# An induced-attention and channel-mix kernel with its transposes, stores and first units in another order

## Chip, cores and metric

The kernel runs on one core of one Trainium2 chip. The metric is the device time of one execution in microseconds (us); the time given is the median of several runs. A core has five engines that run side by side and each work through their own instructions strictly in order: TensorE (PE in the profile; its weight loads are PEld), VectorE (DVE), ScalarE (ACT), GpSimd (POOL) and SyncE (SP), which here issues nearly all DMA transfers. They wait for each other through semaphores.

## What is computed

Two layers follow each other, in float32, for 4 batches of 12608 rows of 128 numbers. The first is attention through 32 inducing rows; the second mixes each row with the row before it and sends the mix through a squared ReLU layer with 1024 hidden channels and a sigmoid gate.

```
mab(q, kv) = softmax(scale * q @ kv.T) @ kv        # scale = 1/sqrt(128)
h    = mab(inducing, x)                            # 32 x 128 for each batch
x1   = mab(x, h)                                   # 12608 x 128
prev = x1 moved down by one row, a row of zeros first
xk   = mu_k * x1 + (1 - mu_k) * prev
xr   = mu_r * x1 + (1 - mu_r) * prev
out  = sigmoid(xr @ w_r) * ((max(xk @ w_k, 0) ** 2) @ w_v)
```

## The kernel before, in words

**Stages.** Stage A makes h of a batch: scores of the inducing rows against x, a running maximum, exponentials, and sums. Stage B makes the attention weights of each row of x against h, 32 per row. It never forms x1: the weights of a row (split in a high and a low part, so that they can be multiplied exactly enough in the fast fp32r form) are laid into a tile R, and h is multiplied into w_k and w_r beforehand (`combine`), which gives the tiles W. One product with W[0] and one with W[1] (R moved by one column, for the previous row) then give the hidden layer.

**Units and steps.** The last layer is cut into groups of 512 rows and each group into 4 units of 256 hidden channels: 25 groups x 4 units x 4 batches = 400 units. The main loop takes one step n for each unit. In step n it issues, on each engine's queue in this order: the gate of a group that is done; `up` of unit n (4 matmuls into the PSUM tile ps_a, lines 839 and 841; there are two such buffers); what stands in `early` for this step (`soon`); `zgate` once per group (lines 828 and 829, the product for the sigmoid); `square` (line 851 on DVE: k_t, the ReLU, which reads ps_a; line 856 on ACT or 853 on DVE: kh, the square rounded to fp32r; line 857 on ACT: the exact square; line 859 on POOL: kl, their difference); `store` of a finished group (line 886 on DVE and line 894, its DMAs); `down` of unit n - 4 (6 matmuls, line 870); and last what stands in `events` for this step (`at`). Only lines 853 and 851 free a ps_a buffer, so `up` of step n waits for them from step n - 2. In steps 4 and 8 of a block of 12 (`high_vector`), line 853 on DVE makes kh instead of ACT.

**What runs beside.** All of stage A of the next batch and stage B of later rows is hung into these steps by hand. For each block of 12 steps that begins at step s there is one `stage_a(b + 1, j, at, s)` and one `stage_b(b, j + 1, at, s + 1)`. With the positions of a block (0 to 11): stage A has the four transposes `btr` (line 359, DVE, they read the loaded x block xb) at positions 9, 11, 0 and 3, each pair followed by a DMA to DRAM (line 362) and by `regroup` DMAs back (line 365) at positions 1 and 5; `load_x` of the next block at 5 (line 207); its scores (line 391, PSUM bank pb_a) at 1, and in the block that also takes in the tail of the batch at 9; the sums over x (`hmm`, line 458, pb_a) at 7 and `acc`, which reads them from pb_a (line 473), at 8. Stage B has its scores (line 649, PSUM bank pb_b) at 1, the transpose and the maximum (`trans` line 656, `maxi` line 659) at 2, the subtraction at 3, and later the exponential, the sum, the division, the way back and the DMAs of `spread` (line 702) into R.

**The start.** `head` makes stage A of batch 0 with no layer to hide behind, and the weights wk, wv and wr are converted from their raw form there (`load_weight`: exponent, mantissa, sign, join; the last has two GpSimd operations). `start` then makes stage B of the first four groups in two parts (`stage_b_head`: scores, turn, diff, expo, norm; then `place`: high, low, put) and the parts of W (`wpart`: product, high on ACT, low on DVE, line 566); what isn't needed by the first unit is hung into steps 0 to 6. W's last columns, for the gate, are `wg`; they are first needed by `zgate(first=True)`, hung into step 4. L537 copies h out of PSUM, L523 makes its factor for k1, L116 is the exponent step of a conversion.

Of the kernel before, what the change touches and what calls it, by code (L numbers as in the profile page):

```python
# [8 lines left out]
F32 = mybir.dt.float32  # L9
# [10 lines left out]
def kernel(  # L20
# [11 lines left out]
    nc = tc.nc  # L32
# [134 lines left out]
    def split_wv(c):  # L167
        cs = slice(c * cg, (c + 1) * cg)
        nc.scalar.copy(out=wvh[:, cs, :], in_=wv_sb[:, cs, :])
        nc.gpsimd.tensor_tensor(out=wvl[:, cs, :], in0=wv_sb[:, cs, :], in1=wvh.bitcast(F32)[:, cs, :],  # L170
                                op=ALU.subtract)

# [165 lines left out]
    def stage_a(b, j, at, t):  # L338
# [130 lines left out]
        def acc():  # L469
# [5 lines left out]
            S.xb.pop(j)  # L475

        for c in range(Q):
            at(t + (-3, -1, 0, 3)[c], lambda c=c: btr(c))
            at(t + (1, 1, 5, 5)[c], lambda c=c: regroup(c))
        if tail:  # L480
# [12 lines left out]
        at(t + 19, t_hmm)  # L493
        at(t + 20, acc)
        k = order_a.index((b, j))
        for bn, jn in order_a[k + 1:]:
            if jn < NBLK - 1:
                at(t + 5, lambda: load_x(bn, jn))
                if jn == NBLK - 2:
                    at(t + 5, lambda: load_x(bn, jt))  # L500
                break


    def combine(b, at=None, t=0):
# [20 lines left out]
        def gates():  # L525
            for nm, mu in (("r0", mur), ("r1", omur)):
                if ahead:
                    h4 = L["h4"][nm] = sm.tile([P, P], F32, name="h4" + nm, bufs=1)
                    nc.scalar.activation(out=h4, in_=L["hp"], func=AF.Copy, scale=mu)
                else:  # L530
                    mixed((nm, mu))

        def hfin():
            ps = pb_tile("a" if ahead else "b")
            nc.tensor.matmul(out=ps[:, :P], lhsT=S.acc, rhs=L["sw"], start=True, stop=True)
            h = sm.tile([P, P], F32, name="hT")
            nc.vector.tensor_copy(out=h, in_=ps[:, :P])  # L537
            S.hT = h[:, :M]
            L["hp"] = ps[:, :P]
            L["h4"] = {}  # L540
            if ahead:
                h4 = L["h4"]["k0"] = sm.tile([P, P], F32, name="h4k0", bufs=1)
                nc.scalar.activation(out=h4, in_=L["hp"], func=AF.Copy, scale=muk)
            else:
                mixed(("k0", muk))
            mixed(("k1", omuk))
            if not ahead:
                gates()
            S.W = [wp.tile([P, WF], F32R, name=f"W{s}") for s in range(2)]
# [81 lines left out]
    def stage_b(b, j, at, t, quick=False):  # L631
# [73 lines left out]
        if quick:  # L705
            at(t, scores)
            for n, f in ((1, trans), (1, maxi), (1, sub), (2, total), (2, recip), (3, mult), (3, back), (4, low)):
                at(t + n, f)
            soon(t + 2, expo)
            soon(t + 4, high)  # L710
            for i in range(Q):
                at(t + 5 + i, lambda i=i: spread(i))
            return
        at(t, scores)
        at(t + 1, trans)
        at(t + 1, maxi)
        at(t + 2, sub)
        at(t + 3, expo)
# [94 lines left out]
    class Group:  # L813
# [62 lines left out]

        def store(self):

# [9 lines left out]
            if g % span == span - 1 or g == NG - 1:  # L888
                o0 = (g % UO - g % span) * G
                t0 = (g - g % span) * G  # L890
                dst = out[self.b, t0:t0 + o - o0 + w, :].rearrange("(s q) (j d) -> j q s d", q=M, d=M)
                for i in range(Q):
                    eng = nc.scalar if self.b == B - 1 and g == NG - 1 and i % 2 else nc.sync
                    eng.dma_start(out=dst[i], in_=ot[M * i:M * (i + 1), o0:o + w]
                                      .rearrange("q (s d) -> q s d", d=M))

# [53 lines left out]
    def head():  # L950
# [52 lines left out]
        for c in range(FC // cg):  # L1003
            split_wv(c)
        spin(5)
# [8 lines left out]
        w.acc()  # L1014
        run(conv["r", 0][:2])
        spin(2)
# [12 lines left out]
    def start():  # L1029
# [15 lines left out]
        def gate_bank(s):  # L1045
            if s == 0:
# [7 lines left out]
        S = batches[0]  # L1054
        run([gates, sc0, sc1, tu0, df0, ex0, wa[0][0], wa[1][0], wb[0][0], lambda: spin(2), tu1, nm0, *conv["r", 0][2:], wa[0][1], hi0,
             wa[1][1], wb[0][1], lo0, wa[0][2], put0, lambda: spin(2),
             df1, ex1, wa[1][2], nm1, hi1])
        for n, f in ((0, wb[1][0]), (0, wb[1][1]), (1, lambda: run([w[0] for w in wg])),
                     (1, sc2), (1, put1)):
            soon(n, f)  # L1060
        for n, f in ((0, lo1), (0, wb[0][2]), (0, wb[1][2]), (2, tu2), (2, df2), (2, ex2), (3, nm2)):
            at(n, f)
        for prod, high, low in wg:
            soon(1, high)
            at(1, low)
        for k, (high, low, put) in enumerate(pl1):
# [26 lines left out]
    with tc.manual_schedule():  # L1093
        head()
        start()
        for n in range(len(units) + LAG + 2):
# [5 lines left out]
            if grp is not None:  # L1102
# [4 lines left out]
                low = grp.square(u, n in high_vector)  # L1107
                low(nc.vector if n == end else nc.gpsimd, 0, grp.w)
            if 1 <= m <= len(units) and units[m - 1][1] == NU - 1:
                units[m - 1][0].store()  # L1110
            if old is not None:
# [32 lines left out]
```

## Time and profile before

| | us |
|---|---|
| median of 3 runs (1113.17 to 1113.67) | 1113.23 |
| profiled execution | 1114.14 |
| its span, first to last instruction | 1111.9 |
| ACT busy in the span | 966.5 |
| POOL busy in the span | 951.7 |

A line of the order of time has the start and the duration in us, the engine, the line of the kernel, the operation, output and inputs, how many such instructions in a row, and in brackets the idle time of the engine before it with what ended it. In the view of waits a line has the engine and the line that waited, the engine and line for which it waited, the total in us, how often, and the longest.

### The profile page before, as it was taken

Reading aid. Unit: us, or ns where it says so; the run is one execution under the profiler, and the core shown is the slowest. Engines: PE = TensorE matmul, PEld = TensorE weight load, DVE = VectorE, ACT = ScalarE, POOL = GpSimd, SP = SyncE. Lnnn points to the kernel's source line nnn. Section 1 sums busy time; section 2 is a strip of 40 time slices with the busy share of each in tenths; the row PEclk is TensorE's granted clock in tenths of the full one; section 3 lists DMA queues with packets and bytes.
Section 4 is the critical chain, followed back from the end, with each engine's and each line's share of the span. In section 5 each row is a group of like instructions: output and inputs, shape, how many; then the busy total and the mean of one; then the engine's idle time right before and its main releaser. Section 6 shows DMA issues by size and latency. Waiting matters only on the chain.

```text
span 1111.9 us, 17188 instructions
## 1 busy us (share of the span) xinstructions
PE 1088.7 (98%) x5723; PEld 832.8 (75%) x5723; DVE 907.3 (82%) x1287; ACT 966.5 (87%) x1098; POOL 951.7 (86%) x417
## 2 busy tenths in 40 slices
PE   8899999999999999999999999999999999999997
PEld 6577777777777777777787777777777787777886
DVE  6988888986878899887778888888676888887665
ACT  6698889889889888888898988979889998999995
POOL 3388998898898988889888999879898899999997
PEclk9999999999999999999999999999999999999999
DMA  9045655661356556653235646655223132232212
GB/s 343 10 127 120 171 147 145 155 167 25 62 135 150 154 148 152 146 152 82 48 78 151 167 119 149 160 138 133 41 55 73 36 66 58 55 70 57 45 29 35
DMA packets 256247, 121.10 MB, mean 109 GB/s; under 512 B 221440, under 2 KB 224672, under 8 KB 253856
## 3 DMA queue, kind: packets, MB, share of 16 engines
q1 hardware_dynamic: 255152, 119.92, 45.2%
q8 instruction: 45, 0.74, 0.3%
q14 instruction: 42, 0.34, 0.1%
q10 hardware_dynamic: 1008, 0.10, 0.1%
HBM read 46.94 MB, written 44.70 MB: 82 GB/s over the span
## 4 chain that ended last, share of the span: by engine, by line
PE 71%; DVE 13%; ACT 4%; issue 3%; DMA 2%; POOL 0%; SPq 0%; DVEq 0%; ACTq 0%; POOLq 0%
PE ps_v L870 35%; PE ps_a L839 14%; PE ps_a L841 13%; DVE k_t L851 6%; PE pb_b L649 2%; ACT kh L856 2%; DVE kh L853 2%; PE pb_a L458 2%; PE pb_a L391 2%; PE ps_v L828 2%; PE ps_v L829 2%; DMA R<-R 1%; DVE s L656 1%; DVE oT L875 1%; ACT k_t L857 1%
## 5 line engine op out<-in xcount | busy, mean ns | idle before, releaser
L859 POOL TENSOR_TENSOR kl<-k_t,kh 128x1024 fp32r<-128x1024 f32 (+1 forms) x399 | 937.3, 2384 | 122.1 <-ACT k_t L857 101.0
L851 DVE TENSOR_SCALAR k_t<-ps_a 128x1024 f32<-128x1024 f32 (+1 forms) x400 | 479.1, 1198 | 142.0 <-PE ps_a L841 115.9
L857 ACT ACTIVATE k_t<-k_t 128x1024 f32<-128x1024 f32 (+1 forms) x400 | 418.4, 1048 | 34.1 <-DVE kh L853 23.0
L856 ACT ACTIVATE kh<-k_t 128x1024 fp32r<-128x1024 f32 (+1 forms) x352 | 365.2, 1038 | 82.7 <-PE ps_v L870 41.6
L839 PE MATMUL ps_a<-R,W 128*128 128x512 f32 (+1 forms) x800 | 323.5, 405 | 8.6 <-DVE k_t L851 4.5
L841 PE MATMUL ps_a<-R,W 128*128 128x512 f32 (+1 forms) x800 | 313.5, 392 | 0.0
L870 PE MATMUL ps_v<-kh,wvh 128*128 128x512 f32 (+1 forms) x800 | 248.4, 391 | 0.0
L870 PE MATMUL ps_v<-kl,wvh 128*128 128x512 f32 (+1 forms) x800 | 247.3, 390 | 0.9 <-POOL kl L859 0.3
L870 PE MATMUL ps_v<-kh,wvl 128*128 128x512 f32 (+1 forms) x800 | 246.8, 390 | 0.0
L839 PEld LDWEIGHTS ps_a<-R,W 128*128 128x128 f32 x800 | 150.8, 188 | 76.7 <-DVE kh L853 10.6
L870 PEld LDWEIGHTS ps_v<-kl,wvh 128*128 128x128 f32 x800 | 148.1, 188 | 38.2 <-POOL kl L859 6.9
L870 PEld LDWEIGHTS ps_v<-kh,wvh 128*128 128x128 f32 x800 | 149.6, 188 | 34.2
L870 PEld LDWEIGHTS ps_v<-kh,wvl 128*128 128x128 f32 x800 | 149.6, 188 | 34.1
L841 PEld LDWEIGHTS ps_a<-R,W 128*128 128x128 f32 x800 | 150.4, 188 | 30.6 <-issue 0.2
L875 DVE TENSOR_TENSOR oT<-ps_v,rT 128x512 f32<-128x512 f32 (+1 forms) x100 | 66.6, 666 | 1.8
L886 DVE STREAM_TRANSPOSE ot<-oT 128x512 f32<-128x512 f32 x96 | 67.2, 700 | 0.0
L853 DVE SCALAR_TENSOR_TENSOR kh<-ps_a,k_t 128x1024 fp32r<-128x1024 f32 x48 | 58.8, 1224 | 5.0
L359 DVE STREAM_TRANSPOSE xs<-xb 128x512 f32<-128x512 f32 x72 | 50.0, 694 | 11.7 <-DMA xb<-in_x_dram 11.7
L831 ACT ACTIVATE rT<-ps_v 128x512 f32<-128x512 f32 (+1 forms) x99 | 57.8, 584 | 0.3
L831 ACT ACT_TABLE_LOAD x31 | 39.8, 1283 | 0.5
L828 PE MATMUL ps_v<-R,W 128*128 128x512 f32 (+1 forms) x99 | 39.1, 395 | 0.4 <-DVE oT L875 0.4
L829 PE MATMUL ps_v<-R,W 128*128 128x512 f32 (+1 forms) x99 | 38.9, 393 | 0.0
(217 smaller groups left out, 607.7 us busy)
## 6 DMA issues: line engine op xcount, KB each, us to landing
out_dram<-ot SPq DMA_DIRECT2D x184, 128.0 KB, 3.3
xb<-in_x_dram SPq DMA_DIRECT2D x18, 1024.0 KB, 6.8
xd<-xs SPq DMA_DIRECT2D x36, 512.0 KB, 3.1
xt<-xd SPq DMA_DIRECT2D x72, 256.0 KB, 4.2
R<-ah SPq DMA_DIRECT2D x184, 64.0 KB, 2.1
R<-al SPq DMA_DIRECT2D x184, 64.0 KB, 2.1
kl<-in_x_dram SPq DMA_DIRECT2D x4, 512.0 KB, 8.8
xb<-in_x_dram SPq DMA_DIRECT2D x4, 512.0 KB, 11.1
```

The source lines that it names most:

```text
L828: nc.tensor.matmul(out=ps[:, :w], lhsT=S.W[0][:, F:WF], rhs=R[:, 1:w + 1], start=True, stop=False)
L831: nc.scalar.activation(out=self.rT, in_=ps[:, :w], func=AF.Sigmoid)
L839: nc.tensor.matmul(out=ps[:, c, :w], lhsT=S.W[0][:, cs], rhs=R[:, 1:w + 1], start=True, stop=False)
L841: nc.tensor.matmul(out=ps[:, c, :w], lhsT=S.W[1][:, cs], rhs=R[:, 0:w], start=False, stop=True)
L851: nc.vector.tensor_scalar(out=k, in0=self.ps[:, :, :w], scalar1=0.0, scalar2=None, op0=ALU.max)
L853: nc.vector.scalar_tensor_tensor(out=kh, in0=self.ps[:, :, :w], scalar=0.0, in1=k, op0=ALU.max, op1=ALU.mult)
L856: nc.scalar.activation(out=kh, in_=k, func=AF.Square)
L857: nc.scalar.activation(out=k, in_=k, func=AF.Square)
L859: return lambda eng, a, z: eng.tensor_tensor(out=kl[:, :, a:z], in0=k[:, :, a:z], in1=kh.bitcast(F32)[:, :, a:z], op=ALU.subtract)
L870: nc.tensor.matmul(out=self.v, lhsT=wt[:, fc, :], rhs=kk[:, c, :], start=(fc == 0 and n == 0), stop=(fc == FC - 1 and n == 2))
L875: nc.vector.tensor_tensor(out=self.oT, in0=self.v, in1=self.rT, op=ALU.mult)
L886: nc.vector.transpose(out=ot[:, o:o + w], in_=self.oT)
```

## The change

Six things change places; the arithmetic is the same, but for who computes two of the factors.

- Stage B: `trans` and `maxi` are issued in the same step as the scores, and `sub` one step earlier. In its quick form (used twice, at the first and second batch's start) the first two also move a step ahead, and all from `total` on comes a step later.
- Stage A: `load_x` is issued before the `btr` and `regroup` of its step; the first `btr` comes a step later (position 10); for the first block of the second batch all `btr` come later (steps 5, 5, 6, 9 in place of 1, 3, 4, 7) and `regroup` two steps later. `acc` comes a step later, at position 9.
- The DMAs of `store` are issued two steps after their transpose, but for the last two groups, which send at once.
- The last unit's kl, on DVE, is issued two steps later.
- In the head, GpSimd's subtraction for wvl and the conversion of wr come later, the factors r0 and r1 are made by GpSimd from h in SBUF, not by ACT from PSUM, and k0 by ACT from SBUF.
- In the start the order is another: the scores of the first part come before the gate factors, W's low parts of the second half come before `lo1`, the gate parts `wg` are multiplied in step 2 (before: 1), and their high and low parts come in step 3 (before: 1).

```diff
--- before.py
+++ after.py
@@ -166,9 +166,14 @@
 
     def split_wv(c):
         cs = slice(c * cg, (c + 1) * cg)
-        nc.scalar.copy(out=wvh[:, cs, :], in_=wv_sb[:, cs, :])
-        nc.gpsimd.tensor_tensor(out=wvl[:, cs, :], in0=wv_sb[:, cs, :], in1=wvh.bitcast(F32)[:, cs, :],
-                                op=ALU.subtract)
+
+        def high():
+            nc.scalar.copy(out=wvh[:, cs, :], in_=wv_sb[:, cs, :])
+
+        def low():
+            nc.gpsimd.tensor_tensor(out=wvl[:, cs, :], in0=wv_sb[:, cs, :], in1=wvh.bitcast(F32)[:, cs, :],
+                                    op=ALU.subtract)
+        return high, low
 
     def groups(j):
 
@@ -474,9 +479,16 @@
                                                in1=L["hp"][:, :C], op0=ALU.mult, op1=ALU.add)
             S.xb.pop(j)
 
+        k = order_a.index((b, j))
+        for bn, jn in order_a[k + 1:]:
+            if jn < NBLK - 1:
+                at(t + 5, lambda: load_x(bn, jn))
+                if jn == NBLK - 2:
+                    at(t + 5, lambda: load_x(bn, jt))
+                break
         for c in range(Q):
-            at(t + (-3, -1, 0, 3)[c], lambda c=c: btr(c))
-            at(t + (1, 1, 5, 5)[c], lambda c=c: regroup(c))
+            at(t + ((1, 1, 2, 5) if t < SEG else (-2, -1, 0, 3))[c], lambda c=c: btr(c))
+            at(t + ((3, 3, 7, 7) if t < SEG else (1, 1, 5, 5))[c], lambda c=c: regroup(c))
         if tail:
             at(t + 5, t_tr)
             soon(t + 11, t_scores)
@@ -491,14 +503,7 @@
         at(t + 19, lambda: hmm(0))
         at(t + 19, lambda: hmm(1))
         at(t + 19, t_hmm)
-        at(t + 20, acc)
-        k = order_a.index((b, j))
-        for bn, jn in order_a[k + 1:]:
-            if jn < NBLK - 1:
-                at(t + 5, lambda: load_x(bn, jn))
-                if jn == NBLK - 2:
-                    at(t + 5, lambda: load_x(bn, jt))
-                break
+        at(t + 21, acc)
 
 
     def combine(b, at=None, t=0):
@@ -526,7 +531,7 @@
             for nm, mu in (("r0", mur), ("r1", omur)):
                 if ahead:
                     h4 = L["h4"][nm] = sm.tile([P, P], F32, name="h4" + nm, bufs=1)
-                    nc.scalar.activation(out=h4, in_=L["hp"], func=AF.Copy, scale=mu)
+                    nc.gpsimd.tensor_tensor(out=h4, in0=L["h"], in1=mu.broadcast_to([P, P]), op=ALU.mult)
                 else:
                     mixed((nm, mu))
 
@@ -536,11 +541,11 @@
             h = sm.tile([P, P], F32, name="hT")
             nc.vector.tensor_copy(out=h, in_=ps[:, :P])
             S.hT = h[:, :M]
-            L["hp"] = ps[:, :P]
+            L["hp"], L["h"] = ps[:, :P], h
             L["h4"] = {}
             if ahead:
                 h4 = L["h4"]["k0"] = sm.tile([P, P], F32, name="h4k0", bufs=1)
-                nc.scalar.activation(out=h4, in_=L["hp"], func=AF.Copy, scale=muk)
+                nc.scalar.activation(out=h4, in_=h, func=AF.Copy, scale=muk)
             else:
                 mixed(("k0", muk))
             mixed(("k1", omuk))
@@ -704,17 +709,17 @@
 
         if quick:
             at(t, scores)
-            for n, f in ((1, trans), (1, maxi), (1, sub), (2, total), (2, recip), (3, mult), (3, back), (4, low)):
+            for n, f in ((0, trans), (0, maxi), (1, sub), (3, total), (3, recip), (4, mult), (4, back), (5, low)):
                 at(t + n, f)
             soon(t + 2, expo)
-            soon(t + 4, high)
+            soon(t + 5, high)
             for i in range(Q):
-                at(t + 5 + i, lambda i=i: spread(i))
+                at(t + 6 + i, lambda i=i: spread(i))
             return
         at(t, scores)
-        at(t + 1, trans)
-        at(t + 1, maxi)
-        at(t + 2, sub)
+        at(t, trans)
+        at(t, maxi)
+        at(t + 1, sub)
         at(t + 3, expo)
         at(t + 5, total)
         at(t + 5, recip)
@@ -874,7 +879,7 @@
             self.oT = mp.tile([P, G], F32, name="oT", bufs=1)[:, :self.w]
             nc.vector.tensor_tensor(out=self.oT, in0=self.v, in1=self.rT, op=ALU.mult)
 
-        def store(self):
+        def store(self, n):
 
             g, w = self.g, self.w
             if g == NG - 1:
@@ -889,10 +894,18 @@
                 o0 = (g % UO - g % span) * G
                 t0 = (g - g % span) * G
                 dst = out[self.b, t0:t0 + o - o0 + w, :].rearrange("(s q) (j d) -> j q s d", q=M, d=M)
-                for i in range(Q):
-                    eng = nc.scalar if self.b == B - 1 and g == NG - 1 and i % 2 else nc.sync
-                    eng.dma_start(out=dst[i], in_=ot[M * i:M * (i + 1), o0:o + w]
-                                      .rearrange("q (s d) -> q s d", d=M))
+                final = self.b == B - 1 and g == NG - 1
+
+                def send():
+                    for i in range(Q):
+                        eng = nc.scalar if final and i % 2 else nc.sync
+                        eng.dma_start(out=dst[i], in_=ot[M * i:M * (i + 1), o0:o + w]
+                                          .rearrange("q (s d) -> q s d", d=M))
+
+                if self.b == B - 1 and g >= NG - 2:
+                    send()
+                else:
+                    at(n + 2, send)
 
 
     def run(th):
@@ -1001,7 +1014,7 @@
         load_x(1, 0)
         w.expo()
         for c in range(FC // cg):
-            split_wv(c)
+            split_wv(c)[0]()
         spin(5)
         v.etrans()
         v.sums()
@@ -1012,7 +1025,6 @@
         weights()
         w.hmm(1)
         w.acc()
-        run(conv["r", 0][:2])
         spin(2)
         hfin()
 
@@ -1052,17 +1064,19 @@
         wg = [wpart(s, None, lambda s=s: gate_bank(s)) for s in range(2)]
         assert F // G == 2
         S = batches[0]
-        run([gates, sc0, sc1, tu0, df0, ex0, wa[0][0], wa[1][0], wb[0][0], lambda: spin(2), tu1, nm0, *conv["r", 0][2:], wa[0][1], hi0,
-             wa[1][1], wb[0][1], lo0, wa[0][2], put0, lambda: spin(2),
-             df1, ex1, wa[1][2], nm1, hi1])
-        for n, f in ((0, wb[1][0]), (0, wb[1][1]), (1, lambda: run([w[0] for w in wg])),
-                     (1, sc2), (1, put1)):
+        wlow = [split_wv(c)[1] for c in range(FC // cg)]
+        rexp, rman, rsign, rjoin = conv["r", 0]
+        run([sc0, gates, rexp, sc1, tu0, df0, ex0, wa[0][0], wa[1][0], wb[0][0], lambda: spin(2), tu1, nm0, wa[0][1],
+             hi0, rman, rsign, wa[1][1], wb[0][1], lo0, put0, lambda: spin(2), wa[0][2], wa[1][2], df1, rjoin, *wlow,
+             ex1, nm1, hi1])
+        for n, f in ((0, wb[1][0]), (0, wb[1][1]), (1, sc2), (1, put1), (2, lambda: run([w[0] for w in wg]))):
             soon(n, f)
-        for n, f in ((0, lo1), (0, wb[0][2]), (0, wb[1][2]), (2, tu2), (2, df2), (2, ex2), (3, nm2)):
+        for n, f in ((0, wb[0][2]), (0, wb[1][2]), (0, lo1),
+                     (2, tu2), (2, df2), (2, ex2), (3, nm2)):
             at(n, f)
         for prod, high, low in wg:
-            soon(1, high)
-            at(1, low)
+            soon(3, high)
+            at(3, low)
         for k, (high, low, put) in enumerate(pl1):
             at(3, high)
             at(4, low)
@@ -1105,9 +1119,12 @@
                 if n >= NU and u == 1:
                     grp.zgate()
                 low = grp.square(u, n in high_vector)
-                low(nc.vector if n == end else nc.gpsimd, 0, grp.w)
+                if n < end:
+                    low(nc.gpsimd, 0, grp.w)
             if 1 <= m <= len(units) and units[m - 1][1] == NU - 1:
-                units[m - 1][0].store()
+                units[m - 1][0].store(n)
+            if n == end + 2:
+                low(nc.vector, 0, units[end][0].w)
             if old is not None:
                 old.down(ou)
             run(events.pop(n, []))
```

## The prediction

> **What bounds the kernel now.** I read the page first, then the waits, then the order of time at the places that the change touches. The page says that TensorE's row is full almost everywhere:
> ```profile
> span 1111.9 us, 17188 instructions
> PE 1088.7 (98%) x5723; PEld 832.8 (75%) x5723; DVE 907.3 (82%) x1287; ACT 966.5 (87%) x1098; POOL 951.7 (86%) x417
> ```
> A busy PE is not a PE at its pace, so the question is where matmuls come later than they could. The waits view names two waits of the matmuls that cost something; both are for DVE to free the PSUM tile ps_a (columns: total us, times, longest):
> ```profile
> PE ps_a L839 <- DVE k_t L851: 4.5, 4, 1.5
> PE ps_a L839 <- DVE kh L853: 3.4, 12, 0.4
> ```
> So the changed order can win only what DVE's lateness costs PE, plus what the two ends of the span hold. One stall of the second kind, in order of time (start, duration); I call units "steps", and count positions 0 to 11 within a block of 12 steps:
> ```profile
> 420.33 1.23 DVE L851 TENSOR_SCALAR k_t<-ps_a 128x1024 f32<-128x1024 f32 x1 [1.34 <-PE ps_a L841]
> ...
> 422.47 0.72 DVE L656 STREAM_TRANSPOSE s<-pb_b 128x512 f32<-128x512 f32 x1
> ...
> 423.22 0.70 DVE L659 TENSOR_REDUCE pb_b<-s 128x16 f32<-128x512 f32 x1
> ...
> 428.07 1.23 DVE L853 SCALAR_TENSOR_TENSOR kh<-ps_a,k_t 128x1024 fp32r<-128x1024 f32 x1
> ...
> 428.43 0.63 PE L870 MATMUL ps_v<-kl,wvh 128*128 128x512 f32 x2
> ...
> 429.35 0.49 PE L839 MATMUL ps_a<-R,W 128*128 128x512 f32 x1 [0.29 <-DVE kh L853]
> ```
> DVE first idles 1.34 us at position 2, then runs stage B's transpose and maximum, arrives late at position 4, where it has k_t and kh to make, and position 6's first matmul waits for kh's end. Two L870 matmuls take 0.63 together and one alone shows 0.40, so the pace is 0.23 and the last matmul's modelled end hides 0.16 of each stall: 429.35 - 428.43 - 2 x 0.23 = 0.46.
>
> **The change, part by part.**
>
> *Stage B's transpose and maximum one step earlier.* They now stand behind the scores (L649) of position 1. Scores end as position 2's matmuls begin, so DVE does this 0.72 + 0.70 in the 1.34 us in which it idled; k_t of position 2 starts up to 0.3 late, and kh of position 4 is ready about 1.1 us sooner, against a lateness of 0.46. The stall should go in every block: 12 times by the row above, 3.4 + 12 x 0.16 = 5.3 us. Bounds: 0 if DVE finds a new wait in their place, 5.3 if none. I take -5.3. The added wait (transpose for scores) holds k_t, store and expo's inputs behind it on DVE; k_t of position 2 has more than a step of slack before ps_a's other buffer is wanted, so nobody is late by 0.3.
>
> *Loads before regroups, stores two steps later, btr of chunk 0 one step later.* The two longest stalls sit where a block's first transpose waits for its x block:
> ```profile
> 477.62 0.62 PE L870 MATMUL ps_v<-kl,wvh 128*128 128x512 f32 x2
> 477.91 0.71 DVE L359 STREAM_TRANSPOSE xs<-xb 128x512 f32<-128x512 f32 x1 [3.31 <-DMA xb<-in_x_dram]
> ...
> 479.79 0.50 PE L839 MATMUL ps_a<-R,W 128*128 128x512 f32 x1 [1.54 <-DVE k_t L851]
> ```
> ```profile
> 748.23 0.49 PE L839 MATMUL ps_a<-R,W 128*128 128x512 f32 x1 [1.11 <-DVE k_t L851]
> ```
> and SP shows why the load was late:
> ```profile
> 458.77 0.34 SPq L362 DMA_DIRECT2D xd<-xs  x1
> 464.15 3.89 SPq L894 DMA_DIRECT2D out_dram<-ot  x4
> 468.13 1.07 SPq L365 DMA_DIRECT2D xt<-xd  x2
> 469.30 0.38 SPq L207 DMA_DIRECT2D xb<-in_x_dram  x1
> ```
> The load is issued behind four stores (which wait for their transpose on DVE) and two regroups. After the change it stands ahead of both, up to 469.30 - 464.15 = 5 us sooner, and its reader comes a step later. Both cover the 3.31 us. Gain: 1.54 + 1.11 + 2 x 0.16 = 3.0 us; if only the step helps, still most of it. What moves on SP: regroups behind a 1 MB load. It is issued about 8.6 us before it is read in these rows (469.30 to 477.91), and a regroup issued behind it is wanted four steps on at the soonest; no loss taken. The stores themselves have two step times more to land and a buffer that is wanted again 12 steps later: nothing.
>
> *acc one step later.* In the block that also takes in the tail, acc falls into the very step in which the tail block's scores want the same bank, pb_a. Before, it was a step ahead:
> ```profile
> 505.86 0.34 DVE L473 SCALAR_TENSOR_TENSOR acc<-acc,alpha,pb_a 128x128 f32<-128x128 f32 x1
> ...
> 506.12 1.22 DVE L851 TENSOR_SCALAR k_t<-ps_a 128x1024 f32<-128x1024 f32 x1
> ...
> 507.25 0.70 DVE L886 STREAM_TRANSPOSE ot<-oT 128x512 f32<-128x512 f32 x1
> 507.38 1.07 PE L391 MATMUL pb_a<-xt,indT 128*32 128x512 f32 x8
> ```
> Now DVE has k_t (from about 505.95, as acc no longer precedes it), the store's transpose, then acc: 505.95 + 1.22 + 0.70 + 0.34 = 508.2 and a semaphore. Scores that started at 507.38 start at 508.3: PE stands 0.9 us, once in each of the three batches that are prepared: +2.7. Bounds 0 (DVE as early as it can be) and 1.3 each (DVE 0.4 later).
>
> *The end.* The last kl (2.10 us on DVE) no longer stands before the last full group's gate and transpose:
> ```profile
> 1102.47 2.10 DVE L859 TENSOR_TENSOR kl<-k_t,kh 128x640 fp32r<-128x640 f32 x1 [1.64 <-ACT k_t L857]
> ...
> 1104.93 0.45 PE L870 MATMUL ps_v<-kl,wvh 128*128 128x320 f32 x2
> ...
> 1106.02 0.49 DVE L875 TENSOR_TENSOR oT<-ps_v,rT 128x320 f32<-128x320 f32 x1
> 1106.55 0.51 DVE L886 STREAM_TRANSPOSE aT<-oT 128x320 f32<-128x320 f32 x1
> ...
> 1107.99 1.10 SPq L894 DMA_DIRECT2D out_dram<-aT  x2
> ```
> PE ends at 1105.38, but the last gate starts at 1106.02, behind the earlier group's gate and transpose; it can start 0.6 sooner. The last stores of SP start 0.9 after the transpose's end (1107.06), behind the earlier group's four DMAs, which now go out long before: together 1107.99 - 1106.5 = 1.5. Bounds -0.6 and -1.5; I take -1.5, since SP's row is the last issue. I leave kl's own end where it is.
>
> *Head and first steps.* The head gets shorter, and then a new wait eats it:
> ```profile
> 38.09 0.49 PE L535 MATMUL pb_a<-mk,acc 128*128 128x128 f32 x2
> ...
> 39.08 0.28 DVE L537 COPY hT<-pb_a 128x128 f32<-128x128 f32 x1
> ...
> 48.00 0.41 DVE L795 TENSOR_TENSOR al<-pb_b,al 128x256 fp32r<-128x256 f32 x1
> 48.45 0.69 DVE L566 TENSOR_TENSOR W<-pb_a,W 64x512 fp32r<-64x512 f32 x1
> ...
> 51.76 0.50 DVE L566 TENSOR_TENSOR W<-ps_v,W 64x128 fp32r<-64x128 f32 x2
> ...
> 53.66 0.47 PE L839 MATMUL ps_a<-R,W 128*128 128x512 f32 x1 [1.39 <-DVE k_t L851]
> ...
> 54.67 0.40 PE L828 MATMUL pb_a<-R,W 128*128 128x512 f32 x1
> ...
> 55.60 0.40 ACT L767 ACTIVATE s<-s 128x256 f32<-128x256 f32 x1
> ...
> 57.34 0.43 DVE L777 TENSOR_TENSOR pb_b<-s,pb_b 128x256 f32<-128x256 f32 x1
> ```
> hT waited 39.08 - 38.58 = 0.5 us for w_r's conversion, which now comes later; the first units start about 0.6 sooner. But the gate weights' low parts (0.50, at 51.76) move to step 3, on DVE behind norm's last operation (L777), which needs the exponentials of step 2 from ACT. PE's first gate product (L828), in step 4, needs those low parts and stands in PE's order before every later matmul. Norm ended at 57.34 + 0.43 = 57.77. The 0.6 from the head is mostly lost on the way, as lo1 (0.41) now comes behind two lows of 0.69 and put1 and its copy on ACT wait for it; I take 0.4 sooner: 57.4, then 0.50: the gate product starts at 57.9 instead of 54.67, +3.2 us. Step 4's own matmuls (53.66) come about 0.7 sooner, which only lengthens the wait: PE is idle some 3.6 us. What is got back: the stalls that PE had until step 16, which with PE later no longer bind, such as
> ```profile
> 77.24 0.47 PE L839 MATMUL ps_a<-R,W 128*128 128x512 f32 x1 [0.43 <-DVE k_t L851]
> ```
> 0.43 + 0.16 there, and about as little elsewhere: +3.2 - 0.9 = +2.3. Bounds: -0.6 (no wait) to +3.2. The gates' factors go from ACT to GpSimd, and wvl's subtraction to behind the conversion, in a stretch where GpSimd has no other work: nothing. The first batch's four transposes and the quick stage B move by a step or more into steps that, with PE later, have the time; their rows of R are due at step 16, five steps after the last of them is made: nothing.
>
> **Sum:** -5.3 - 3.0 + 2.7 - 1.5 + 2.3 = -4.8. The span of 1111.9 becomes 1107.1; the profiled execution took 1114.14, 0.9 above the median of 1113.23, and against the median the forecast is 1108.4. I count as the same what lies within 0.2% (2.2 us, about what a measurement of this kernel can tell): 1111.0 to 1115.4.
>
> **Rivals.**
>
> *The gate product does not wait* (ACT's exponentials come so early that norm and the lows are done by step 4, or PE has other work). Against it: L777 ended 3.1 us after L828 began. Time: -4.8 - 2.9 = 1105.5. Chance 0.12.
>
> *The idle of 3.6 us costs clock.* The granted clock in windows over the end (third figure from the end of each line):
> ```profile
> 1107.00:1108.00 1.00, 0.00 (x0) 0.00 (x0) 0.06 (x1) 0.00 (x0) 0.00 (x0) 1.00 0.74 117
> 1108.00:1109.00 1.00, 0.00 (x0) 0.00 (x0) 0.00 (x0) 0.00 (x0) 0.00 (x0) 0.83 0.99 142
> ```
> After PE's last matmul (1105.38) the clock fell within 1108 to 1109: 0.83 is one third of that microsecond at half, so 3.3 us after. A gap of 3.6 us in step 4 is just long enough. If matmuls then run at half speed for as long again, 3.3 us of work are 1.6 us late: 1110.0. [...] Chance 0.12.
>
> *Slower: DVE's queue becomes the bound.* The transpose waits at the head of DVE's queue for scores that PE issues last in its step; if it holds k_t of position 2 more than about 0.7 us beyond what I count, kh of position 4 is as late as before and -5.3 is lost: 1113.7. From there every further 0.1 us per block costs 0.1 x 15 blocks: 0.3 more is +4.5, 1118.2. Against it:
> ```profile
> 87.20:219.60 132.40, 131.22 (x698) 98.59 (x697) 118.33 (x164) 114.17 (x128) 114.54 (x49) 1.00 0.59 149
> ```
> in four blocks (87.2 to 219.6) DVE's busy time, the third of the busy times, is 118.33 of 132.40: 3.5 us a block are free. For it: DVE serves in order, so free time at the wrong place is worth nothing. Chance 0.12, half of it above 1115.4.
>
> **Chances.** The forecast 0.64, with its own range 1106 to 1111 from the bounds of acc (0 to 1.3 each), end and head. Faster by over 0.2% has nine tenths of the forecast, the first rival and most of the second: 0.78; the same 0.14; slower 0.08. The range 1104.2 to 1112.8 leaves out the far ends of the first and the third rival.
>
> **What would show it.** Right: the wait of L839 on kh L853 down from 12 times to 3 or fewer; no wait of xs on the x load over 1 us; a wait of L391 for acc three times, near 0.8 each; L828's first row near 58, with PE idle before it and the low parts (L566, 64x128) just before; the last SP store about 1.5 us nearer to PE's last matmul. Wrong: blocks of 12 steps still 33.1 us long (132.40 / 4), or a first gate product on time.

## The result, and the profile after

| | us | runs |
|---|---|---|
| before, median | 1113.45 (1113.17 to 1114.73) | 4 |
| after, median | 1104.92 (1104.70 to 1105.09) | 4 |
| after, profiled execution | 1105.09, its span 1103.3 | |

The ratio is 0.9921, 95% interval [0.9904, 0.9938]: the change takes 8.5 us away, where 5.1 (against this median) were forecast. Line numbers of the kernel after are 5 higher than before for most lines (839 is 844, 870 is 875), 8 for the stores (894 is 902). First the head of the page after, and its chain of work that ended last, by engine:

```profile
span 1103.3 us, 17166 instructions
PE 1083.2 (98%) x5723; PEld 837.2 (76%) x5723; DVE 911.1 (83%) x1287; ACT 967.4 (88%) x1096; POOL 952.9 (86%) x419
...
PE 91%; DVE 4%; ACT 2%; issue 1%; POOL 1%; DMA 1%; POOLq 0%; SPq 0%; DVEq 0%; ACTq 0%
```

TensorE has the same 5723 matmuls and a share of 98% as before; its busy time says nothing of the gain. The waits do:

```profile
DVE s L661 <- PE pb_b L654: 12.0, 24, 1.2
...
PE pb_a L833 <- DVE W L571: 3.2, 1, 3.2
...
PE ps_a L844 <- DVE kh L858: 0.3, 1, 0.3
```

The twelve waits for kh are one. No matmul waits for k_t any more, and no transpose of x waits for its load. In their place stand two new ones: DVE waits 24 times for stage B's scores (first line, the wait that the change added), behind which no matmul is seen to wait, and TensorE waits once, 3.2 us, for the gate's low parts. (A third new wait, for acc, stands in the view under another name; its experiment below shows it.) The block shown before looks like this in the order of time (the steps are those of 420.33 to 429.35 before):

```profile
418.28 0.72 DVE L661 STREAM_TRANSPOSE s<-pb_b 128x512 f32<-128x512 f32 x1 [0.17 <-PE pb_b L654]
419.03 0.69 DVE L664 TENSOR_REDUCE pb_b<-s 128x16 f32<-128x512 f32 x1
419.64 1.21 DVE L856 TENSOR_SCALAR k_t<-ps_a 128x1024 f32<-128x1024 f32 x1
...
426.02 1.22 DVE L858 SCALAR_TENSOR_TENSOR kh<-ps_a,k_t 128x1024 fp32r<-128x1024 f32 x1
```

DVE works without a gap from 418.28 to k_t, where it had idled 1.34 us and then been late. kh is done at 427.24, and the first matmul of position 6, due near 428.0, finds the buffer free.

Where the 8.6 us of the span went, from the starts of the steps' first matmuls in the two traces:

| | before | after | difference |
|---|---|---|---|
| step 0 | 45.48 | 44.82 | -0.66 |
| step 4 | 53.66 | 52.99 | -0.67 |
| step 5 | 56.54 | 60.40 | +3.86 |
| step 16 | 87.21 | 90.99 | +3.78 |
| step 160 | 479.79 | 476.11 | -3.68 |
| step 399 | 1099.15 | 1091.11 | -8.04 |
| end of the span | 1111.9 | 1103.3 | -8.6 |

So the start loses 3.8, steps 16 to 399 win 11.8, and the end wins 0.6. The traced execution of the kernel before took 1114.14, 0.7 above its median, so the spans differ by a little more than typical ones do. On the other side the device time goes beyond the span by 2.2 us before and by 1.8 after: 0.4 of the 8.5 lies outside the span, and no run here shows why.

### The profile page after: what moved, and what is told of

Read it like the earlier page. It is cut to its first block, busy times and chain, and to the rows that moved or that the text cites. A ratio compares the mean times of both kernels' runs of the same rounds, so it can differ in the third digit from the quotient of the medians.

```text
span 1103.3 us, 17166 instructions
## 1 busy us (share of the span) xinstructions
PE 1083.2 (98%) x5723; PEld 837.2 (76%) x5723; DVE 911.1 (83%) x1287; ACT 967.4 (88%) x1096; POOL 952.9 (86%) x419
## 4 chain that ended last, share of the span: by engine, by line
PE 91%; DVE 4%; ACT 2%; issue 1%; POOL 1%; DMA 1%; POOLq 0%; SPq 0%; DVEq 0%; ACTq 0%
PE ps_v L875 47%; PE ps_a L844 17%; PE ps_a L846 16%; PE ps_v L833 2%; PE pb_b L654 2%; PE ps_v L834 2%; PE pb_a L463 2%; PE pb_a L396 2%; ACT kh L861 1%; POOL kl L864 1%; DVE k_t L856 1%; DMA xl<-in_x_dram 1%; DVE mx L263 0%; PE pb_a L583 0%; ACT k_t L862 0%
## 5 line engine op out<-in xcount | busy, mean ns | idle before, releaser
L836 ACT ACTIVATE rT<-ps_v 128x512 f32<-128x512 f32 (+1 forms) x99 | 57.9, 585 | 0.4
```

The source lines that it names most:

```text
L836: nc.scalar.activation(out=self.rT, in_=ps[:, :w], func=AF.Sigmoid)
```

## The experiments

**Theory:** DVE's order in the blocks was the bound; stage B's transposes win most of the time, the loads some, and acc and the gate product give some of it back. **Rivals:** the gain comes from the loads and stores and the transposes are only along; or the start's new order wins and the wait in it is only seen. Each kernel starts from the kernel after, unless it is said otherwise. The ratios are against the kernel before, which was timed again beside them in three groups: its median was 1112.83 us beside the transposes (undone, and alone), acc and the early gate product, 1113.25 beside loads and stores both undone, the filled wait, the old start and all together, and 1112.78 beside the last three (stores at once, load put back, all four stores on SP). The kernel after was timed only beside 1113.45, so a difference from its 1104.92 is uncertain by up to 0.7 us, the spread of these medians.

**The transposes: undone, and done alone.** Undone in the kernel after:

```diff
-        at(t, trans)
-        at(t, maxi)
-        at(t + 1, sub)
+        at(t + 1, trans)
+        at(t + 1, maxi)
+        at(t + 2, sub)
```

> The changed kernel with stage B's transpose, maximum and subtraction one step later again (not in the quick form). Theory: the stall of position 6 (0.46 us, and 0.1 at the restart) comes back in each full block and the blocks between batches lose too: blocks of 33.0 in place of 32.5, in all 6 to 9 us more, 1111 to 1114. Rival: the gain is of the earlier loads and later stores, and the blocks stay at 32.5: within 1.5 us of 1104.9.

Measured: 1114.18 (10 runs, 1113.97 to 1115.72), ratio 1.0011 [1.0002, 1.002]. Without this one part the change is no gain at all, and its trace has the old wait back (13 times in the view of waits):

```profile
PE ps_a L844 <- DVE kh L858: 3.7, 13, 0.3
```

The same three lines the other way round, as the only edit of the kernel before:

```diff
-        at(t + 1, trans)
-        at(t + 1, maxi)
-        at(t + 2, sub)
+        at(t, trans)
+        at(t, maxi)
+        at(t + 1, sub)
```

> The kernel before with stage B's transpose, maximum and subtraction one step earlier (not in the quick form) and nothing else. Theory: full blocks of 32.5 in place of 33.1, the two waits for the x load stay (34.7 and 34.3 become about 34), no gate stall: 6 to 8 us less than 1113.4, 1105.5 to 1107.5. Rival: the blocks need the later stores, too, and the time falls by less than 2.

Measured: 1102.91 (1101.75 to 1105.22), ratio 0.9913 [0.9898, 0.9928]. Three lines alone win 9.9 us, more than the whole change and more than the 1105.5 to 1107.5 expected. The first rival falls. Of the two long stalls for an x load only one is left in its profiled execution (the 1105.22), and it is a costly one:

```profile
736.30 0.71 DVE L359 STREAM_TRANSPOSE xs<-xb 128x512 f32<-128x512 f32 x1 [4.06 <-DMA xb<-in_x_dram]
...
738.18 0.50 PE L839 MATMUL ps_a<-R,W 128*128 128x512 f32 x1 [1.82 <-DVE k_t L851]
...
739.41 1.05 PE L870 MATMUL ps_v<-kh,wvh 128*128 128x512 f32 x2
```

The last row shows two matmuls in 1.05 where 0.63 is usual: the granted clock was 0.98 in the window 738 to 739, 0.50 from 739 to 742 and 0.82 in 742 to 743, so it was at half from 738.96 to 742.37. Stall and clock together would make a spread of 3.5 us if they come in some executions and not in others; only this one was traced.

**Loads and stores: both undone, and each.** The load behind the regroups, the first transpose a step earlier and the stores at once:

```diff
-        k = order_a.index((b, j))
...
-            at(t + ((1, 1, 2, 5) if t < SEG else (-2, -1, 0, 3))[c], lambda c=c: btr(c))
+            at(t + ((1, 1, 2, 5) if t < SEG else (-3, -1, 0, 3))[c], lambda c=c: btr(c))
...
+        k = order_a.index((b, j))
...
-                if self.b == B - 1 and g >= NG - 2:
-                    send()
-                else:
-                    at(n + 2, send)
+                send()
```

> The changed kernel with the x loads behind the regroups again, the first btr a step earlier again, and the stores sent at once. Theory of the prediction: the waits of btr for the x load come back (they cost 3.0 us at steps 160 and 260 before): about 1107.9. Rival, after the run in which only stage B was moved (1101.75 to 1105.22, one such wait in its profile): the earlier transposes on DVE end most of those waits by themselves, the time rises by 0 to 2 and spreads by some us from run to run.

Measured: 1106.69 (6 runs, 1105.43 to 1108.93), ratio 0.9942 [0.9926, 0.9958], 1.8 us above the kernel after and spread over 3.5 us, where that has 0.4. (The slowest, 1108.93, had a granted clock of 0.945, the others 0.997, so the top of this spread may have another cause.) The wait is back:

```profile
DVE xs L364 <- DMA xb<-in_x_dram: 12.3, 6, 3.6
```

Then the stores alone sent at once (the last five lines of this diff):

> The changed kernel with the stores sent at once again; the loads' place and the later first transpose stay as changed. Of the 1.8 us that undoing loads and stores together cost: if the loads' place alone is what takes the wait for the x block away, this kernel is within 0.4 us of the changed one and shows no wait of xs for the x load over 1 us. Rival: the four stores ahead of the load on SP are what made it late, wherever the load stands in its step; then the stalls near 476 and 742 are back and it is 1 to 2 us slower.

And the load and the first transpose alone put back (the lines above them):

> The changed kernel with the load behind the regroups and the first transpose one step earlier again; the stores stay two steps later. If the loads' place is what counts, the stalls near 476 and 742 are back and it is 1 to 2 us slower than the changed kernel; if the stores are, it is within 0.4 us of it. If each alone suffices, both this kernel and the one with the stores at once stay within 0.4 us.

Measured: stores at once 1105.92 (1105.03 to 1106.92), ratio 0.9938 [0.9926, 0.9951]; load put back 1104.80 (1104.64 to 1105.74), 0.9929 [0.9917, 0.9942]. In neither trace is there a wait for the x load: either edit alone removes it. But the first has a new wait, at 251.36, where the tail block's scores are due:

```profile
PE pb_a L396 <- DMA xt<-xd: 1.8, 1, 1.8
```

The regroups, now behind four stores and a 1 MB load, land too late for the scores: the load lands at 249.83, the two regroups at 250.56 and 251.22. In the kernel after they land at 246.14 and 246.88, and the same scores stand 0.58 us. So with the stores two steps later the load's place brings nothing that the runs show (1104.80 against 1104.92). With the load first, the stores' delay is worth 1.0 by the medians, little more than that uncertainty; the traces put 1.2 into the one block of this wait (steps 64 to 76 take 35.64 against 34.39 in the kernel after) and almost nothing into the other blocks.

**acc one step earlier again:**

```diff
-        at(t + 21, acc)
+        at(t + 20, acc)
```

> The changed kernel with acc one step earlier again (as before the change). Theory: the three waits of the tail block's scores (L396, 0.74 us each at 249.1, 504.3 and 768.7) go and nothing takes their place: 2.2 us less, about 1102.7. Rival: acc at the earlier place delays k_t after the kh step on DVE by 0.35 us in each of some 15 blocks, and the time stays at 1104.9 or rises by up to 2.

Measured: 1102.82 (1102.68 to 1102.91), ratio 0.9909 [0.9893, 0.9926]: 2.1 us less than the kernel after. The three blocks with a tail show why; here the second of them in the kernel after:

```profile
503.24 0.70 DVE L891 STREAM_TRANSPOSE ot<-oT 128x512 f32<-128x512 f32 x1
503.86 0.30 DVE L478 SCALAR_TENSOR_TENSOR acc<-acc,alpha,pb_a 128x128 f32<-128x128 f32 x1
```
```profile
503.07 0.62 PE L875 MATMUL ps_v<-kl,wvh 128*128 128x512 f32 x2
504.27 1.07 PE L396 MATMUL pb_a<-xt,indT 128*32 128x512 f32 x8 [0.57 <-PE ps_v L875]
```

acc ends at 504.16 and the scores start 0.11 later. Their start is 0.74 us late (504.27 - 503.07 - 2 x 0.23), three times. The profile names TensorE's own product as releaser; the order of time and the experiment name acc.

**The gate product: earlier, and its wait filled.** The view of the start in the kernel after:

```profile
53.77 0.39 PE L846 MATMUL ps_a<-R,W 128*128 128x512 f32 x1
57.41 0.49 PE L833 MATMUL pb_a<-R,W 128*128 128x512 f32 x1 [3.25 <-DVE W L571]
58.02 0.88 PE L875 MATMUL ps_v<-kh,wvh 128*128 128x512 f32 x2
58.69 1.05 PE L875 MATMUL ps_v<-kh,wvl 128*128 128x512 f32 x2
```
```profile
56.60 0.43 DVE L782 TENSOR_TENSOR pb_b<-s,pb_b 128x256 f32<-128x256 f32 x1
57.06 0.50 DVE L571 TENSOR_TENSOR W<-ps_v,W 64x128 fp32r<-64x128 f32 x2
```

The low parts stand behind norm's last operation, as forecast. After the wait the matmuls run at about half pace (two take 0.88, then 1.05, where 0.63 is usual), and the windows show the granted clock at 0.50 (third figure from the end):

```profile
57.00:58.00 1.00, 0.59 (x2) 0.48 (x3) 0.94 (x4) 1.00 (x2) 1.00 (x1) 1.00 0.00 0
58.00:59.00 1.00, 1.00 (x4) 0.82 (x3) 0.97 (x2) 0.98 (x4) 1.00 (x2) 0.60 0.00 0
...
61.00:62.00 1.00, 1.00 (x5) 0.79 (x4) 0.00 (x0) 0.97 (x2) 0.00 (x0) 0.69 0.00 0
```

The gate's products, high and low parts back in step 1:

```diff
-        for n, f in (..., (1, sc2), (1, put1), (2, lambda: run([w[0] for w in wg]))):
+        for n, f in (..., (1, lambda: run([w[0] for w in wg])), (1, sc2), (1, put1)):
...
-            soon(3, high)
-            at(3, low)
+            soon(1, high)
+            at(1, low)
```

> The changed kernel with the gate parts of W (product, high, low) back in step 1. Theory: PE's wait of 3.25 us before the first gate product (L833) and the clock at half from 58.2 to 61.6 both come from the low parts standing behind norm on DVE in step 3; both go, 3.3 + 1.7 = 5 us less some 1 us of stalls that come back: about 1101, and step 16 begins 4 us sooner than the changed kernel's 90.99. Rival: the steps to 16 are bound by ACT and DVE anyway (ACT was busy nearly without a gap there before), and the time stays within 1 us of 1104.9.

Measured: 1101.87 (1101.64 to 1101.99), ratio 0.9901 [0.9886, 0.9916], 3.05 less than the kernel after; the wait is gone, the granted clock of the profiled execution is 0.999 (0.997 in the kernel after), and step 5 starts at 56.05. The second rival falls: the wait is paid for. To split the wait from the clock, the wait stays and 24 products of the identity fill it; they add matmuls that nobody reads:

```diff
+        soon(4, lambda: spin(12, bank().rearrange("p (a n) -> p a n", a=2)))
```

> The changed kernel with 24 dummy matmuls of 128 columns (2.6 us, results not used) between the matmuls of step 4 and the first gate product, so that PE has work in the 3.25 us in which it stands. Theory: the wait itself stays (first gate product near 57.4) but the clock is not cut at 58.2, so the matmuls after it run at 0.23 and not 0.43: 1.6 us less than 1104.9, 1103.3. Rival: the clock falls for another reason than the idle time, or what it costs is hidden behind ACT: within 0.5 us of 1104.9.

Measured: 1103.30 (1103.15 to 1103.45), ratio 0.991 [0.9895, 0.9925], 1.6 less than the kernel after.

```profile
53.95 2.84 PE L960 MATMUL ps_v<-ident 128*128 128x128 f32 x24
57.37 0.50 PE L833 MATMUL pb_a<-R,W 128*128 128x512 f32 x1 [0.57 <-DVE W L571]
57.97 0.63 PE L875 MATMUL ps_v<-kh,wvh 128*128 128x512 f32 x2
```

The gate product starts as late as before (57.37), the pair of matmuls behind it takes 0.63 in place of 0.88, and the granted clock of the execution is 0.999. So the clock costs 1.6 and the wait itself the rest of the 3.05. The starts of step 16 agree: 90.99 in the kernel after, 89.39 with the wait filled, 87.68 with the gate parts early.

**The change without its start.** The kernel before, with the transposes, the loads first, the later first transpose, the later stores and the later last kl, but the old head, start, quick form and acc. Of its diff against the kernel after, three of the parts that are put back:

```diff
-        at(t + 21, acc)
+        at(t + 20, acc)
...
-            for n, f in ((0, trans), (0, maxi), (1, sub), (3, total), (3, recip), (4, mult), (4, back), (5, low)):
+            for n, f in ((1, trans), (1, maxi), (1, sub), (2, total), (2, recip), (3, mult), (3, back), (4, low)):
...
-            soon(3, high)
-            at(3, low)
+            soon(1, high)
+            at(1, low)
```

> The change without its head, start, quick form and acc: the kernel before with stage B's transpose and maximum in the scores' step, the loads first, the first btr a step later, the later stores and the later last kl. Theory: the new head and start cost 3.8 us by step 16 and acc 2 us, so this is 5.5 to 6 us under the changed kernel: 1099. Rival: the head's gain of 0.7 us is real and only the gate parts are wrong: then this is slower than the changed kernel with the gate parts and acc put back (about 1099.8 as the sum of two runs).

Measured: 1100.47 (1100.42 to 1101.01), ratio 0.9886 [0.9871, 0.9901]. It is 4.45 us faster than the whole change: the other half of the diff makes the kernel slower. In its trace steps 16 to 399 take 998.82 us against 1011.94 before, so transposes, loads and stores together win 13.1 there. The 1099 expected was missed by 1.5, though the span (1097.9) is 5.4 shorter than the changed kernel's: the time beyond the span is 2.5 us here, a part that the traces don't explain. The old start reaches step 16 at 87.36, the new one with early gate parts at 87.68: but for the gate parts, the new start is neither much worse nor a gain.

**All that helped together.** The kernel after with the early gate parts, acc at its old place, `lo1` ahead of the two lows, the quick form's `low` one step later, and SP given the first two of the last four stores:

```diff
-            for n, f in (..., (4, mult), (4, back), (5, low)):
+            for n, f in (..., (4, mult), (4, back), (6, low)):
...
-                        eng = nc.scalar if final and i % 2 else nc.sync
+                        eng = nc.scalar if final and i >= 2 else nc.sync
...
-        for n, f in ((0, wb[0][2]), (0, wb[1][2]), (0, lo1),
+        for n, f in ((0, lo1), (0, wb[0][2]), (0, wb[1][2]),
```

> The changed kernel with the gate parts in step 1, acc a step earlier, lo1 ahead of W's low parts again, the quick form's low one step later, and the last four stores shared so that SP has the first two and ACT the last two. Theory: the costs add up: 3.0 (gate and clock, as measured), 2.1 (acc, as measured), about 1 (steps 1 and 13), 1 to 1.5 (SP's last store no longer waits for ACT's first to land): 1097.5 to 1099. Rival: PE meets ACT's or GpSimd's limit in the first steps, and only 5 of it are seen: 1100.

Measured: 1096.42 (1096.16 to 1096.49), ratio 0.9848 [0.9833, 0.9863], 8.5 us below the kernel after. The gate parts and acc gave 3.05 and 2.1 alone; the other 3.3 lie with `lo1` and `low`, more than the 1 us expected. They weren't tried apart, but the traces show two waits of TensorE that the kernel with only the gate parts early has, and this one hasn't:

```profile
PE ps_v L833 <- DVE oT L880: 1.2, 1, 1.2
...
PE pb_b L753 <- DVE al L800: 1.1, 1, 1.1
```

The second is `lo1`: behind W's two lows it reads the bank that the next scores (L753) want, and step 5 starts at 56.05 instead of 54.95. The first is the quick form's `low`: a step too early in DVE's queue, it stands there for ACT's `high` and holds oT behind it, and from step 13 to step 14 it takes 4.79 us instead of 2.79. In the kernel after, the same `low` idles DVE by 1.33:

```profile
82.43 0.69 DVE L698 TENSOR_TENSOR al<-pb_b,ah 128x512 fp32r<-128x512 f32 x1 [1.33 <-ACT ah L694]
```

The part at the end failed: SP's second store still came late.

```profile
1089.42 2.41 SPq L902 DMA_DIRECT2D out_dram<-aT  x2
```

In the trace the two issues begin at 1089.42 and 1091.51. The kernel after has its second one as late (1098.49 and 1100.44); there the view of SP's waits names a store from aT:

```profile
SPq L902 <- DMA out_dram<-aT: 1.6, 1, 1.6
```

In its trace that issue waits on semaphore 108, the one that ACT's first store (1098.49) carries; that store landed at 1100.42. That the same holds here was my estimate from those times. With all four on SP:

```diff
-                        eng = nc.scalar if final and i >= 2 else nc.sync
+                        eng = nc.sync
```

> The version with the early gate parts, the earlier acc and lo1 first, but all of the last four stores on SP. If SP's second last store is late because it shares a completion semaphore with a store on ACT, four in a row on SP go out at 0.3 to 0.55 us each from the transpose's end, the last about 1.0 to 2.2 us after the first, and the span ends 0.3 to 1.2 us nearer to PE's last matmul than the 6.05 us of the version with two stores on each: 1095.2 to 1096.1. Rival: the store itself takes that long to be issued on SP in this place; then the four take over 3 us and the end is no nearer, 1096.4 or later.

```profile
1089.95 1.82 SPq L902 DMA_DIRECT2D out_dram<-aT  x4
```

Four go out in less time than two did, and the span ends 5.5 us after the last matmul, not 6.1. The total is 1095.70 (1095.50 to 1096.09), ratio 0.9846 [0.9832, 0.9859]: by the interval it can't be told from the version with two stores on each queue; only the tail of the trace is shorter.

## Why the prediction was right, and where its terms were off

The sign, the stated range and the mechanism held. The measured 1104.92 lies below the narrower 1106 to 1111 that the forecast gave as its own, and next to the 1105.5 of the first rival, whose condition did not come true. Against the -8.6 of the span the sum of -4.8 is 3.8 short: transposes, load waits, acc and blocks that had no term came out 6.2 better than written, start and end 2.4 worse. That such errors partly cancelled is luck.

- **Transposes, -5.3: the mechanism was right, the term too small.** The 12 full blocks (steps 16 to 64, 100 to 148, 200 to 248) win 7.8 in all, 0.65 each, where I had 0.28 + 0.16 = 0.44. The step that failed is "the last matmul's modelled end hides 0.16 of each stall": I counted the late first matmul of position 6 and not the one behind it. In the trace of before it is 0.10 late as well, in each of these blocks, as here (0.33 behind the first, where the pace is 0.23):

```profile
429.35 0.49 PE L839 MATMUL ps_a<-R,W 128*128 128x512 f32 x1 [0.29 <-DVE kh L853]
429.68 0.39 PE L841 MATMUL ps_a<-R,W 128*128 128x512 f32 x1
```

  Position 6 lost 6.2 us in the twelve (1.2 of it by second matmuls), and loses nothing after; the other 1.6 are smaller delays at positions 0, 9, 10 and 11, as 0.23 at 120.27, which I had left out.
- **Loads and stores, -3.0: the two blocks win 4.1 (2.3 and 1.8), but the credit was put wrongly.** The transposes alone already clear the first of them. "The stores themselves ... nothing" is the step that fails: with the stores at once the kernel loses about 1.0, with the load put back nothing. The load's place matters only where the stores stand before it. And a regroup behind a 1 MB load, for which I took no loss, does come late when the stores stand ahead of both (1.8 us, once).
- **acc, +2.7:** 0.74 three times in the trace, 2.1 by the experiment. I had 0.9 each. DVE's order was the forecast one (k_t, the store's transpose, acc); I had added up durations, and in these rows each instruction starts about 0.08 before the one ahead of it has ended by its duration. My sign for it ("a wait of L391 for acc") was not to be seen in the view of waits, which names another releaser.
- **The end, -1.5:** -0.6, the lower bound. The two steps that I counted came: the last gate starts 0.04 after TensorE's last matmul ends at 1097.38 (before 0.64), and the first stores go out 0.03 after the transpose's end (SP's before 0.93). What I had not asked is when SP's second one can go.

```profile
1097.42 0.49 DVE L880 TENSOR_TENSOR oT<-ps_v,rT 128x320 f32<-128x320 f32 x1 [0.85 <-PE ps_v L875]
1097.95 0.51 DVE L891 STREAM_TRANSPOSE aT<-oT 128x320 f32<-128x320 f32 x1
1098.49 2.27 SPq L902 DMA_DIRECT2D out_dram<-aT  x2
1098.49 0.89 ACTq L902 DMA_DIRECT2D out_dram<-aT  x2
```

  Of the two that the third row counts, the second begins at 1100.44 in the trace, when the first of ACT's has landed (1100.42). Before, both were out in 1.10; at that pace it could go at 1099.04, 1.4 sooner.
- **Head and start, +2.3:** the gate product came at 57.41 (forecast 57.9) after an idle of 3.25 (forecast 3.6), behind norm's last operation as written. With the wait filled, step 16 is 2.19 later than before, 0.1 from the term; but that includes a cost that I had put at nothing ("the quick stage B ... nothing"): its `low` makes step 13 take 3.67 us where it took 2.81, so the closeness is in part luck. In the kernel after it is 3.78, since the second rival came true as well: the idle cost the clock for 3.41 us, 1.6 us of time. I gave that 0.12, from the 3.3 us at the end of the kernel before; the last section has four traces with this wait, and half clock in all four.
- **Rivals.** The gate product did wait. DVE's queue did not become the bound: it waits 24 times for the scores, at most 1.2 us, and no matmul waits for k_t.
- The blocks that hold neither a full stage B nor a long stall win another 1.7 in all, for which the prediction had no term; I have not taken them apart. The later last kl and the moves of GpSimd's and ACT's work in the head were not tried alone either.

Sum by the trace: +3.8 (start) - 7.8 (full blocks) - 4.1 (load waits) + 1.8 (the three blocks with acc, as far as their length shows it) - 1.7 - 0.6 = -8.6.

## What to carry to other kernels

Here a reader of PSUM that was put directly behind its producer cost the bounding engine nothing, since its own engine idled at that moment, and what it won was felt steps later, at the buffer that came free in time; price such a stall with the late matmul behind it as well. Try each part of a large reordering alone: here three lines were worth more than the whole diff, and half of it cost 4.5 us. An operation hung one step too early in DVE's queue held what stood behind it: `low` held oT, and TensorE waited 1.2 us for oT. The late operation at the start of the main loop was paid for twice, by its wait and by 1.6 us for the clock.

## What the runs showed of the hardware

**Half clock came behind idle time of TensorE.** Five traces show it in the main loop, by the granted clock in their windows; the idle time begins with the end of the last matmul before it:

| kernel | TensorE idle | first at half | at half for |
|---|---|---|---|
| after | 54.16 to 57.41 (3.25) | 58.20 | 3.41 |
| loads and stores both undone | 53.77 to 57.00 (3.23) | 57.18 | 3.4 |
| stores at once | 53.98 to 57.21 (3.23) | 56.42 | 6.8 |
| load put back | 53.63 to 56.87 (3.24) | 56.18 | 6.83 |
| transposes alone | 736.36 to 738.18 (1.82) | 738.96 | 3.41 |

Two windows of the kernel with the load put back, beside those of the kernel after above:

```profile
56.00:57.00 1.00, 0.13 (x1) 0.13 (x1) 0.93 (x4) 0.97 (x2) 1.00 (x1) 0.59 0.00 0
...
62.00:63.00 1.00, 1.00 (x3) 0.72 (x3) 0.53 (x1) 0.00 (x0) 0.89 (x1) 0.50 0.00 0
```

That profiled execution took 1105.74, and the median of its kernel 1104.80. In the table half clock begins 2.4 to 4.0 us after TensorE had stopped, in two of the five before it had work again. Behind the last matmul it begins after 3.3 us in the kernel before (1105.38 to 1108.66) and after 1.9 in the kernel after (1097.38 to 1099.27). These shorter idle times had full clock behind them: 1.60 us before 49.41 in the kernel after, at full clock from 7.00 to 58.20, and 1.39, 1.54 and 1.11 before 53.66, 479.79 and 748.23 in the kernel before, at full clock from 6.15 to 1108.66. What decides when the clock falls and for how long was not shown. My prediction had the 3.3 us alone to go by and took a gap of 3.6 as "just long enough"; gaps of 3.2 were followed by half clock in four traces of four, and so was one of 1.82.

**The matmul behind a stall came late too.** In the kernel before the second matmul follows 0.33 or 0.34 us behind the first at the twelve waits of position 6 and at the two long ones (479.79 and 748.23), where the pace is 0.23. Behind the wait of 0.71 at 311.45 in the kernel after it follows by 0.25.

**A store on SP waited for one on ACT.** SP's second one of the last four stores stood 1.6 us for a store from aT in the kernel after, and began 0.02 after ACT's first had landed (1100.44 and 1100.42); with SP given the first two it began 2.09 after the first (1089.42 and 1091.51). The four in a row on SP went out in 1.82 us. In the kernel before the same two stores on SP were out in 1.10.
